# Gated FFN on one core: x loaded in halves of the model dimension, first weights in small pieces in order of use

## The chip, the cores and the metric

The kernel runs on one core of a Trainium2 chip. A core has a matrix engine (TensorE, PE in the profile), a vector engine (VectorE, DVE), a scalar engine (ScalarE, ACT), GpSimd (POOL) and a sync engine (SP). Each runs its own program in order, and they wait for each other on semaphores. Transfers between HBM and the on-chip memory (SBUF) are issued by SP, ACT or POOL, and are carried out by 16 DMA engines. Matrix products go into PSUM, eight banks of 512 fp32 columns on 128 partitions.

The metric is the device time of one execution in microseconds (us). Before the change it is 301.58 us, the median of three runs (301.4 to 301.84).

## The reference

A gated feed-forward layer in bf16: 1024 tokens (B x S = 32 x 32), model dimension D = 1024, hidden dimension F = 3584.

```python
def reference(x, w_gate, w_up, w_down):
    return (_gelu(x @ w_gate) * (x @ w_up)) @ w_down
```

`_gelu` is the tanh approximation. x is 2 MB; the three weights are 7.3 MB each.

## The kernel before

**Layout.** D is cut into 8 pieces of 128 (`dk`), F into 28 chunks of 128 (`m`). PE needs the contraction on the partitions, so x has to be transposed (`xT`); weights are used as they lie. The rows of D are dealt to partitions as d = 8p + k: partition p of piece k holds row 8p + k of the weights, and x is transposed to match.

**x.** x arrives in three pieces by tokens, A (0 to 256), B (256 to 512) and C (512 to 1024). `load_x` (L263) loads a piece in four DMAs, one for each quarter of D on its own 32 partitions, in rows of 256 elements (512 bytes). Two quarters go by SP's queue and two by ACT's. The staging area `xs` lies in the part of `hT` that is written last. DVE then makes each `dk` piece of `xT` with one 32x32-block transpose (L402), which reads every eighth element. It can't begin before both queues have delivered the piece.

**First weights.** Chunks 0 to 7 of both weights (`wgbig`, `wubig`) come row by row (L269): k = 0 and 1 as 128 x 512 pieces, shared between the queues, k = 2 to 7 as 128 x 1024, gate on SP and up on ACT. `early_loads` writes the order: A, weights k = 0 to 7, B, C; 16 DMAs on each queue. On ACT these issues stand ahead of every GELU in the program; only the load of the function's table and one small activation are ahead of them.

**Later weights.** `load_w` (L257) loads groups of four chunks, 1 MB each, gate by SP and up by POOL. `gate_w` holds each until its buffer is free; the first group waits for the whole of x. `issue_wd` (L251) loads `w_down` in the same two programs.

**Order on PE.** Nine dummy matmuls on constants (L324) run first. Then PE goes through *parts* (L345): a part is one chunk m with one stretch of tokens, and needs 8 gate and 8 up matmuls. Parts 0 to 7 are chunks 0 to 7 on tokens A, parts 8 to 15 the same chunks on B, each with 256 columns; gate and up of a part share one PSUM bank (part 8 takes the bank of part 0, and so on). The other 48 have 512 columns. `together` interleaves: for parts 0 to 7 it goes through dk = 0 to 5 for all eight, then finishes them one by one with dk 6 and 7; for parts 8 to 11 it does dk = 0 to 4 for all four, then finishes them; the others go one by one. A matmul waits for its weights, for its transposed x and, where the bank was used, for the product that empties it.

**Order on ACT and DVE.** ACT takes the GELU of the gate half (L383) into one of four buffers. DVE multiplies it with the up half into `hT` (L409); this is called E0, E1 and so on after the part. DVE's order is written out by hand: eight transposes of A, then products and transposes of B and C in the order of `mix`:

`E0 E1 B0 E2 B1 E3 B2 E4 B3 E5 B4 E6 B5 E7 B6 B7 C0 E8 C1 ...`

The second product, hT times `w_down` (L367), follows on PE; ACT and DVE copy its results out in turn (L389, L415) and SP stores them (L313).

Of the kernel before, what the change touches and what calls it, by code (L numbers as in the profile page):

```python
# [5 lines left out]
P = 128  # L6
# [78 lines left out]
def bass_standalone__geglu_ffn__sampling_kernel(  # L85
# [7 lines left out]
    xf = x.flatten_outer_dims()  # L93
# [5 lines left out]
    DK = D // P  # L99
# [21 lines left out]

    XC = N // 32
    XE = D // 4
    XA, XB, XC2 = (0, 256), (256, 512), (512, 1024)
    XPIECES = [XA, XB, XC2]
    W0 = [(0, 0, 512), (0, 512, 1024), (1, 0, 512), (1, 512, 1024)]
    W0 += [(k, 0, 1024) for k in range(2, DK)]

    parts = []
    for t0, t1 in (XA, XB):
# [7 lines left out]
    NPART = len(parts)  # L142
# [10 lines left out]

    steps = []

    def together(ps_, ks):
        for dk in range(ks):
            for key in ("G", "U"):
                for p in ps_:
                    steps.append((p, key, dk))  # L160
        for p in ps_:
            for key in ("G", "U"):
                for dk in range(ks, DK):
                    steps.append((p, key, dk))

    together(range(0, 8), 6)
    together(range(8, 12), 5)
    for p in range(12, NPART):
        together([p], 0)


    dve_order = [("T", dk) + XA for dk in range(DK)]
    mix = "E0 E1 B0 E2 B1 E3 B2 E4 B3 E5 B4 E6 B5 E7 B6 B7 C0 E8 C1 E9 C2 E10 E11 C3 C4 E12 C5 E13 C6 E14 C7 E15"
    for w in mix.split():
        if w[0] == "E":
            dve_order.append(("E", int(w[1:])))
        else:
            dve_order.append(("T", int(w[1:])) + (XB if w[0] == "B" else XC2))
    dve_order += [("E", p) for p in range(NSHORT, NPART)]

    jobs = []
# [14 lines left out]
    wu_r = w_up.rearrange("(p k) f -> p k f", k=DK)  # L196
# [6 lines left out]
    Q_X = {(q, s): _Clock(f"x{i}{s}", 16) for i, q in enumerate(XPIECES) for s in range(2)}  # L203
    Q_W0 = {(w, p): _Clock(f"{w}0k{p[0]}c{p[1]}", 16) for p in W0 for w in ("wg", "wu")}
# [8 lines left out]
    ctx = _Ctx()  # L213

    with ExitStack() as es:
# [38 lines left out]
        def load_w(ew, eng, w, j):  # L254
            c0, gsz, buf = groups[j]
            q = (Q_WG if w == "wg" else Q_WU)[j]
            ctx.set((w, j), ew.do(lambda: eng.dma_start(  # L257
                wbuf(w, buf)[:, :, 0:gsz * P], w_r[w][:, :, c0 * P:(c0 + gsz) * P]), clock=q))

        def load_x(ew, eng, q, side):  # L260
            c0, c1 = q[0] // 32, q[1] // 32
            for a in (2 * side, 2 * side + 1):
                v = ew.do(lambda: eng.dma_start(  # L263
                    xs[32 * a:32 * (a + 1), c0:c1, :], x_r[a, :, c0:c1, :]), clock=Q_X[(q, side)])
            ctx.set(("x", q, side), v)

        def load_w0(ew, eng, w, p):
            k, f0, f1 = p
            ctx.set((w + "0", p), ew.do(lambda: eng.dma_start(  # L269
                big[w][:, k, f0:f1], w_r[w][:, k, f0:f1]), clock=Q_W0[(w, p)]))  # L270

        def early_loads(ew, eng, side):
            load_x(ew, eng, XA, side)
            for k in range(2):
                for w in ("wg", "wu"):
                    load_w0(ew, eng, w, W0[2 * k + side])
            for k in range(2, DK):
                load_w0(ew, eng, ("wg", "wu")[side], W0[2 + k])
            load_x(ew, eng, XB, side)
            load_x(ew, eng, XC2, side)  # L280

        def gate_w(ew, j):
            if war[j] is None:
                for s in range(2):
                    ew.wait(Q_X[(XC2, s)], ctx.get(("x", XC2, s)))
                return -1
            ew.wait(C_PE, ctx.get(("U", last_part[war[j]])))
            return war[j]
# [26 lines left out]
                    osb[:, tc, col0:col0 + ncols]), clock=Q_OUT)  # L315
            sp.wait(Q_OUT, last)

        NDUMMY = 9

        def prog_pe(eng):  # L320
            pe = _Eng(ctx, eng, C_PE)
            v = None
            for i in range(NDUMMY):
                v = pe.do(lambda: eng.matmul(ps[:, 7, :], ones_w, ones_x,  # L324
                                             start=True, stop=True), mark=(i == NDUMMY - 1))
            pe.wait(C_PE, v)
            opened = set()
            for (i, key, dk) in steps:
                m, t0, t1, gs, us = parts[i]
                w, (bank, f0, f1) = ("wg", gs) if key == "G" else ("wu", us)  # L330
                buf, slot, j = slot_of[m]
                if j is None:
                    p = next(p for p in W0 if p[0] == dk and p[1] <= m * P < p[2])
                    pe.wait(Q_W0[(w, p)], ctx.get((w + "0", p)))
# [4 lines left out]
                for q in XPIECES:  # L339
                    if q[0] < t1 and t0 < q[1]:  # L340
                        pe.wait(C_DVE, ctx.get(("T", dk, q)))
# [3 lines left out]
                v = pe.do(lambda: eng.matmul(  # L345
                    ps[:, bank, f0:f1],
                    wbuf(w, buf)[:, dk, slot * P:(slot + 1) * P],
                    xT[:, dk, t0:t1],
                    start=first, stop=last and (key == "U" or gs[0] != us[0]),
                ), mark=last)  # L350
                if last:
                    ctx.set((key, i), v)
            pe.wait(Q_WD_SP, ctx.get("wd_sp_total"))
            pe.wait(Q_WD_POOL, ctx.get("wd_pool_total"))
            bank_last_job = {}
            for ji, (tc, col0, ncols, b) in enumerate(jobs):
                if b in bank_last_job:
                    pj = bank_last_job[b]
                    pe.wait(C_ACT if evac_eng_is_act(pj) else C_DVE, ctx.get(("E", pj)))
                else:  # L360
                    pe.wait(C_DVE, ctx.get(("D", owner[b])))
                bank_last_job[b] = ji
                v = None
                for m in range(FM):
                    pe.wait(C_DVE, ctx.get(("D", last_part[m])))
                    last = (m == FM - 1)
                    v = pe.do(lambda: eng.matmul(  # L367
                        ps[:, b, 0:ncols],
                        hT[:, m, tc * P:(tc + 1) * P],
                        wd[:, m, col0:col0 + ncols],  # L370
                        start=(m == 0), stop=(m == FM - 1),
                    ), mark=last)
                ctx.set(("O", ji), v)
# [18 lines left out]
        def prog_dve(eng):  # L392
            dve = _Eng(ctx, eng, C_DVE)

            for what in dve_order:
                if what[0] == "T":
                    dk, q = what[1], what[2:]
                    for s in range(2):
                        dve.wait(Q_X[(q, s)], ctx.get(("x", q, s)))
                    src = xs[:, q[0] // 32:q[1] // 32, :].rearrange(  # L400
                        "p c (j k) -> p c j k", k=DK)[:, :, :, dk]
                    ctx.set(("T", dk, q), dve.do(lambda: eng.transpose(  # L402
                        xT[:, dk, q[0]:q[1]].rearrange("p (c i) -> p c i", i=32), src)))
                else:
                    i = what[1]
                    m, t0, t1, _gs, (ub, u0, u1) = parts[i]
                    dve.wait(C_ACT, ctx.get(("A", i)))
                    dve.wait(C_PE, ctx.get(("U", i)))
                    ctx.set(("D", i), dve.do(lambda: eng.tensor_tensor(  # L409
                        hT[:, m, t0:t1], t_bufs[i % NTB][:, 0:t1 - t0], ps[:, ub, u0:u1], ALU.mult)))  # L410
# [56 lines left out]
```

## Time and profile before

| What | Value |
|---|---|
| median of three runs | 301.58 us (301.4 to 301.84) |
| the profiled execution | 300.94 us |
| its span, first to last instruction | 299.6 us |
| PE busy | 294.0 us, 98% of the span |
| DVE busy | 60.2 us |
| ACT busy | 41.4 us |
| moved by DMA | 26.43 MB, mean 88 GB/s |
| first 22.5 us: DMA busy tenths of three slices | 8, 9, 9 |
| granted TensorE clock | 1.00 |

In the timeline a row gives the start, the time taken, the engine, the line, the operation with output and input, the count, and in brackets how long the engine was idle before it and what released it. SPq and ACTq rows are the issuing of DMAs, not the transfer. In the table by stretches a row gives the stretch in us, its length, the busy share of PE, PEld, DVE, ACT and POOL with the instructions begun, the TensorE clock, the busy share of the DMA engines (which can pass 1, as transfers on one engine overlap) and their GB/s.

### The profile page before, as it was taken

What the parts mean: (1) busy time and instruction counts of PE and PEld (TensorE: products, weight loads), DVE (VectorE), ACT (ScalarE), POOL (GpSimd) and SP (SyncE); (2) the same over time, 40 slices, a digit from 0 to 9 for tenths busy, and PEclk for the clock granted to TensorE, in tenths of its full rate; (3) what the DMA queues carried; (4) which work ended last, traced back from release to release, by engine and by line L of the source; (5) the groups of instructions that cost most, each with busy time, mean ns of one, the idle gap of its engine ahead of it and who ended that gap; (6) DMA issues with size and microseconds to landing.
All of it is one profiled execution on the core that took longest, in us unless ns stands there. A gap on an engine that the chain in (4) does not pass through costs nothing.

```text
span 299.6 us, 3392 instructions
## 1 busy us (share of the span) xinstructions
PE 294.0 (98%) x1485; PEld 147.6 (49%) x1509; DVE 60.2 (20%) x96; ACT 41.4 (14%) x75; POOL 7.0 (2%) x12
## 2 busy tenths in 40 slices
PE   7999999999999999999999999999999999999997
PEld 3878744444444444444444444444444444444456
DVE  3259811211111211111211112210000000000000
ACT  1042211111211111211111211110000000000000
POOL 0001001020001002000000000000000000000000
DMA  8998002947007400952103000000000100010001
GB/s 239 381 223 270 13 1 81 343 142 278 2 0 251 171 0 7 357 198 63 77 0 142 0 0 2 0 0 18 20 18 18 35 20 18 18 36 19 18 18 37
DMA packets 19118, 26.43 MB, mean 88 GB/s; under 512 B 1056, under 2 KB 13472, under 8 KB 19104
## 3 DMA queue, kind: packets, MB, share of 16 engines
q1 hardware_dynamic: 13344, 14.68, 15.0%
q0 software_dynamic: 2176, 8.39, 7.9%
q10 hardware_dynamic: 3584, 3.15, 3.4%
q8 instruction: 12, 0.20, 0.3%
q14 instruction: 2, 0.02, 0.0%
HBM read 24.12 MB, written 2.10 MB: 87 GB/s over the span
## 4 chain that ended last, share of the span: by engine, by line
PE 97%; DMA 1%; issue 1%; DVE 1%; ACT 0%; DVEq 0%
PE ps L345 64%; PE ps L367 32%; DMA hT<-in_x_dram 1%; DVE xT L402 0%; ACT L377 0%; DVE hT L409 0%; ACT xT L389 0%; DVEq L41 0%
## 5 line engine op out<-in xcount | busy, mean ns | idle before, releaser
L367 PE MATMUL ps<-wd,hT 128*128 128x512 bf16 (+1 forms) x468 | 96.5, 366 | 0.4
L345 PE MATMUL ps<-xT,wgbig 128*128 128x512 bf16 (+1 forms) x378 | 78.6, 343 | 1.8 <-DVE xT L402 0.8
L345 PE MATMUL ps<-xT,wubig 128*128 128x512 bf16 (+1 forms) x379 | 78.8, 343 | 0.3
L367 PEld LDWEIGHTS ps<-wd,hT 128*128 128x128 bf16 x476 | 46.6, 98 | 50.4
L409 DVE TENSOR_TENSOR hT<-tb,ps 128x512 bf16<-128x512 f32 (+1 forms) x64 | 39.1, 613 | 140.8 <-PE ps L345 140.6
L383 ACT ACTIVATE tb<-ps 128x512 f32<-128x512 f32 (+1 forms) x64 | 34.8, 544 | 162.7 <-PE ps L345 161.2
L345 PEld LDWEIGHTS ps<-xT,wgbig 128*128 128x128 bf16 x384 | 37.4, 98 | 34.6 <-PE ps L324 1.7
L345 PEld LDWEIGHTS ps<-xT,wubig 128*128 128x128 bf16 x384 | 37.6, 98 | 31.9 <-DMA wubig<-in_w_up_dram 0.3
L345 PE MATMUL ps<-xT,wgsmall 128*128 128x512 bf16 x126 | 30.1, 379 | 0.1
L345 PE MATMUL ps<-xT,wusmall 128*128 128x512 bf16 x125 | 29.8, 379 | 0.2
L415 DVE CAST xT<-ps 128x512 bf16<-128x512 f32 (+1 forms) x8 | 5.3, 658 | 88.1 <-PE ps L367 88.1
L345 PEld LDWEIGHTS ps<-xT,wusmall 128*128 128x128 bf16 x128 | 12.5, 98 | 15.1
L345 PEld LDWEIGHTS ps<-xT,wgsmall 128*128 128x128 bf16 x128 | 12.5, 98 | 15.1
L402 DVE STREAM_TRANSPOSE xT<-hT 128x256 bf16<-128x256 bf16 (+1 forms) x24 | 17.8, 771 | 5.9 <-DMA hT<-in_x_dram 5.9
L389 ACT ACTIVATE xT<-ps 128x512 bf16<-128x512 f32 (+1 forms) x9 | 5.2, 573 | 93.1 <-PE ps L367 93.1
L324 PE MATMUL ps<-const-bfloat16-1.0 128*128 128x512 bf16 x9 | 4.0, 629 | 0.8 <-PEq L452 0.8
L257 POOL DMA_DIRECT2D wubig<-in_w_up_dram x3 | 2.6, 883 | 64.8 <-PE ps L345 64.8
L257 POOL DMA_DIRECT2D wusmall<-in_w_up_dram x2 | 1.9, 960 | 48.5 <-PE ps L345 26.0
L251 POOL DMA_DIRECT2D wd<-in_w_down_dram x3 | 2.3, 762 | 19.1 <-PE ps L345 19.1
L324 PEld LDWEIGHTS ps<-const-bfloat16-1.0 128*128 128x128 bf16 x9 | 1.2, 141 | 2.7 <-issue 2.7
L377 ACT ACT_TABLE_LOAD x1 | 1.3, 1283 | 0.7 <-PEq L452 0.7
L377 ACT ACTIVATE warm<-const-float32-0.0 128x1 f32<-128x1 f32 x1 | 0.2, 202 | 0.0
(4 smaller groups left out, 0.4 us busy)
## 6 DMA issues: line engine op xcount, KB each, us to landing
wd<-in_w_down_dram SPq DMA_DIRECT2D x4, 1024.0 KB, 10.6
wgbig<-in_w_gate_dram SPq DMA_DIRECT2D x3, 1024.0 KB, 5.6
wubig<-in_w_up_dram POOLq DMA_DIRECT2D x3, 1024.0 KB, 9.5
wd<-in_w_down_dram POOLq DMA_DIRECT2D x3, 1024.0 KB, 10.1
wgsmall<-in_w_gate_dram SPq DMA_DIRECT2D x2, 1024.0 KB, 5.6
wusmall<-in_w_up_dram POOLq DMA_DIRECT2D x2, 1024.0 KB, 8.8
out_dram<-xT SPq DMA_DIRECT2D x15, 128.0 KB, 1.7
wgbig<-in_w_gate_dram SPq DMA_DIRECT2D x6, 256.0 KB, 7.6
```

What stands on the lines that cost most here:

```text
L251: ew.do(lambda: eng.dma_start(wd[:, a:b, :], wd_r[:, a:b, :]), clock=clock)
L257: ctx.set((w, j), ew.do(lambda: eng.dma_start(wbuf(w, buf)[:, :, 0:gsz * P], w_r[w][:, :, c0 * P:(c0 + gsz) * P]), clock=q))
L324: v = pe.do(lambda: eng.matmul(ps[:, 7, :], ones_w, ones_x, start=True, stop=True), mark=(i == NDUMMY - 1))
L345: v = pe.do(lambda: eng.matmul(ps[:, bank, f0:f1], wbuf(w, buf)[:, dk, slot * P:(slot + 1) * P], xT[:, dk, t0:t1], start=first, stop=last ...
L367: v = pe.do(lambda: eng.matmul(ps[:, b, 0:ncols], hT[:, m, tc * P:(tc + 1) * P], wd[:, m, col0:col0 + ncols], start=(m == 0), stop=(m == F ...
L377: act.do(lambda: eng.activation(warm[:, 0:1], const0, ACTF.Gelu_apprx_tanh))
L383: ctx.set(("A", i), act.do(lambda: eng.activation(t_bufs[i % NTB][:, 0:t1 - t0], ps[:, gb, g0:g1], ACTF.Gelu_apprx_tanh)))
L389: ctx.set(("E", ji), act.do(lambda: eng.activation(osb[:, tc, col0:col0 + ncols], ps[:, b, 0:ncols], ACTF.Copy)))
L402: ctx.set(("T", dk, q), dve.do(lambda: eng.transpose(xT[:, dk, q[0]:q[1]].rearrange("p (c i) -> p c i", i=32), src)))
L409: ctx.set(("D", i), dve.do(lambda: eng.tensor_tensor(hT[:, m, t0:t1], t_bufs[i % NTB][:, 0:t1 - t0], ps[:, ub, u0:u1], ALU.mult)))
L415: ctx.set(("E", ji), dve.do(lambda: eng.tensor_copy(osb[:, tc, col0:col0 + ncols], ps[:, b, 0:ncols])))
```

## The change

Five things are changed together.

- Rows of D are dealt in two halves, d = 512 hh + 4p + k: pieces dk = 0 to 3 need only the first half of x's columns, 4 to 7 the second. x comes in six pieces (three stretches of tokens by two halves) in rows of 128 elements, 256 bytes. There are 24 DMAs for x where there were 12.
- The first weights follow a written list, `EARLY`. k = 0 and 1 come in pieces of 512 columns, the first and last of them halved by partitions over both queues; k = 2 to 5 come as whole rows, each halved by partitions (64 x 1024 on each queue); k = 6 and 7 come together in four pieces of 128 x 2 x 512. The second half of A comes between k = 3 and k = 4; B and C come at the end. Each queue issues 27 early DMAs.
- PE's order: for dk 0 and 1, parts 0 to 3 and then 4 to 7; dk 2 to 5 for all eight; then parts 0 to 3 do dk 6 and are finished one by one, and parts 4 to 7 likewise. Parts 8 to 11 do dk 0 to 4 as before.
- DVE's order has four products ahead of the first transpose of B.
- Eight dummy matmuls; `load_w` loads each group in two DMAs.

The core of the diff:

```diff
-    XA, XB, XC2 = (0, 256), (256, 512), (512, 1024)
-    XPIECES = [XA, XB, XC2]
-    W0 = [(0, 0, 512), (0, 512, 1024), (1, 0, 512), (1, 512, 1024)]
-    W0 += [(k, 0, 1024) for k in range(2, DK)]
+    T_A, T_B, T_C = (0, 256), (256, 512), (512, 1024)
+    XPIECES = [t + (hh,) for t in (T_A, T_B, T_C) for hh in range(2)]
+    LO, HI, ALL = (0, 512), (512, 1024), (0, 1024)
+    EARLY = [("x", XPIECES[0]),
+             ("w", "wg", (0, 1), LO, (0, 1)), ("w", "wu", (0, 1), LO, (0,)), ("w", "wg", (0, 1), HI, (1,)),
+             ("w", "wu", (0, 1), HI, (0,)), ("w", "wg", (1, 2), LO, (1,)),
+             ("w", "wu", (1, 2), LO, (0,)), ("w", "wg", (1, 2), HI, (1,)),
+             ("w", "wu", (1, 2), HI, (0, 1))]
+    for k in (2, 3):
+        EARLY += [("w", "wg", (k, k + 1), ALL, (0, 1)), ("w", "wu", (k, k + 1), ALL, (0, 1))]
+    EARLY += [("x", XPIECES[1])]
+    for k in (4, 5):
+        EARLY += [("w", "wg", (k, k + 1), ALL, (0, 1)), ("w", "wu", (k, k + 1), ALL, (0, 1))]
+    EARLY += [("w", "wg", (6, 8), LO, (0,)), ("w", "wu", (6, 8), LO, (1,)),
+              ("w", "wg", (6, 8), HI, (0,)), ("w", "wu", (6, 8), HI, (1,))]
+    EARLY += [("x", q) for q in XPIECES[2:]]
...
-    together(range(0, 8), 6)
-    together(range(8, 12), 5)
-    for p in range(12, NPART):
-        together([p], 0)
-    dve_order = [("T", dk) + XA for dk in range(DK)]
-    mix = "E0 E1 B0 E2 B1 E3 B2 E4 B3 E5 B4 E6 B5 E7 B6 B7 C0 E8 C1 E9 C2 E10 E11 C3 C4 E12 C5 E13 C6 E14 C7 E15"
+    first, second = range(0, 4), range(4, 8)
+    for dk in (0, 1):
+        run(first, [dk])
+        run(second, [dk])
+    run(range(0, 8), range(2, 6))
+    for ps_ in (first, second):
+        run(ps_, [6])
+        for p in ps_:
+            run([p], [7])
+    run(range(8, 12), range(0, 5))
+    for p in range(8, NPART):
+        ks = range(5 if p < 12 else 0, DK)
+        run([p], ks, ("G",))
+        run([p], ks, ("U",))
+    dve_order = []
+    for w in ("A0 A1 A2 A3 A4 A5 A6 A7 E0 E1 E2 E3 B0 B1 E4 B2 E5 B3 E6 E7 B4 B5 B6 B7 "
+              "C0 E8 C1 E9 C2 E10 C3 E11 C4 E12 C5 E13 C6 E14 C7 E15").split():
...
-    x_r = xf.rearrange("(c i) (a e) -> a i c e", i=32, a=4)
-    wg_r = w_gate.rearrange("(p k) f -> p k f", k=DK)
+    x_r = xf.rearrange("(c i) (hh a e) -> hh a i c e", i=32, hh=2, a=4)
+    wg_r = w_gate.rearrange("(hh p k) f -> p hh k f", hh=2, k=KH)
...
         def early_loads(ew, eng, side):
+            for it in EARLY:
+                if it[0] == "x":
+                    t0, t1, hh = q = it[1]
+                    for a in (2 * side, 2 * side + 1):
+                        v = ew.do(lambda: eng.dma_start(
+                            xs[32 * a:32 * (a + 1), t0 // 32:t1 // 32, hh * 128:(hh + 1) * 128],
+                            x_r[hh, a, :, t0 // 32:t1 // 32, :]), clock=Q_X[(q, side)])
+                    ctx.set(("x", q, side), v)
+                elif side in it[4]:
+                    _, w, (k0, k1), (f0, f1), sides = it
+                    p0, p1 = (0, P) if len(sides) == 1 else (64 * side, 64 * side + 64)
+                    ctx.set((it, side), ew.do(lambda: eng.dma_start(
+                        big[w][p0:p1, k0:k1, f0:f1],
+                        w_r[w][p0:p1, k0 // KH, k0 % KH:k0 % KH + k1 - k0, f0:f1]),
+                        clock=Q_W0[(it, side)]))
...
-        NDUMMY = 9
+        NDUMMY = 8
```

`run(ps_, ks, keys)` appends, for each dk in `ks`, the gate matmuls of the parts and then their up matmuls.

More of the change, by code (lines that the diff above doesn't have):

```diff
@@ L120, in bass_standalone__geglu_ffn__sampling_kernel @@
     wd_gate_chunk = [min(FM - 1, 3 + 3 * k) for k in range(len(wd_groups))]
+    KH = DK // 2
     XC = N // 32
     XE = D // 4
-    XA, XB, XC2 = (0, 256), (256, 512), (512, 1024)
-    XPIECES = [XA, XB, XC2]
-    W0 = [(0, 0, 512), (0, 512, 1024), (1, 0, 512), (1, 512, 1024)]
-    W0 += [(k, 0, 1024) for k in range(2, DK)]
+    T_A, T_B, T_C = (0, 256), (256, 512), (512, 1024)
[14 more added lines that the diff above has]
+    EARLY += [("x", q) for q in XPIECES[2:]]
     parts = []
-    for t0, t1 in (XA, XB):
+    for t0, t1 in (T_A, T_B):
         for m in range(NBIG):
@@ L154, in bass_standalone__geglu_ffn__sampling_kernel, with run @@
     steps = []
-    def together(ps_, ks):
-        for dk in range(ks):
-            for key in ("G", "U"):
+    def run(ps_, ks, keys=("G", "U")):
+        for dk in ks:
+            for key in keys:
                 for p in ps_:
                     steps.append((p, key, dk))
-        for p in ps_:
-            for key in ("G", "U"):
-                for dk in range(ks, DK):
-                    steps.append((p, key, dk))
-    together(range(0, 8), 6)
-    together(range(8, 12), 5)
-    for p in range(12, NPART):
-        together([p], 0)
-    dve_order = [("T", dk) + XA for dk in range(DK)]
-    mix = "E0 E1 B0 E2 B1 E3 B2 E4 B3 E5 B4 E6 B5 E7 B6 B7 C0 E8 C1 E9 C2 E10 E11 C3 C4 E12 C5 E13 C6 E14 C7 E15"
-    for w in mix.split():
+    first, second = range(0, 4), range(4, 8)
[5 more added lines that the diff above has]
+        run(ps_, [6])
+        for p in ps_:
+            run([p], [7])
[7 more added lines that the diff above has]
+              "C0 E8 C1 E9 C2 E10 C3 E11 C4 E12 C5 E13 C6 E14 C7 E15").split():
         if w[0] == "E":
@@ L177, in bass_standalone__geglu_ffn__sampling_kernel @@
         else:
-            dve_order.append(("T", int(w[1:])) + (XB if w[0] == "B" else XC2))
+            dve_order.append(("T", int(w[1:])) + {"A": T_A, "B": T_B, "C": T_C}[w[0]])
     dve_order += [("E", p) for p in range(NSHORT, NPART)]
@@ L193, in bass_standalone__geglu_ffn__sampling_kernel @@
     out_r = of.rearrange("(tc p) d -> p tc d", p=P)
-    x_r = xf.rearrange("(c i) (a e) -> a i c e", i=32, a=4)
-    wg_r = w_gate.rearrange("(p k) f -> p k f", k=DK)
-    wu_r = w_up.rearrange("(p k) f -> p k f", k=DK)
+    x_r = xf.rearrange("(c i) (hh a e) -> hh a i c e", i=32, hh=2, a=4)
+    wg_r = w_gate.rearrange("(hh p k) f -> p hh k f", hh=2, k=KH)
+    wu_r = w_up.rearrange("(hh p k) f -> p hh k f", hh=2, k=KH)
     wd_r = w_down.rearrange("(m p) d -> p m d", p=P)
@@ L202, in bass_standalone__geglu_ffn__sampling_kernel @@
     C_POOL = _Clock("pool")
-    Q_X = {(q, s): _Clock(f"x{i}{s}", 16) for i, q in enumerate(XPIECES) for s in range(2)}
-    Q_W0 = {(w, p): _Clock(f"{w}0k{p[0]}c{p[1]}", 16) for p in W0 for w in ("wg", "wu")}
+    Q_X = {(q, e): _Clock(f"x{i}{e}", 16) for i, q in enumerate(XPIECES) for e in range(2)}
+    Q_W0 = {(it, e): _Clock(f"{it[1]}k{it[2][0]}c{it[3][0]}q{e}", 16)
+            for it in EARLY if it[0] == "w" for e in it[4]}
     Q_WG = [_Clock(f"wg{j}", 16) for j in range(NG)]
@@ L256, in load_w @@
             q = (Q_WG if w == "wg" else Q_WU)[j]
[L257 to L270, printed above, removed]
-        def early_loads(ew, eng, side):
[L273 to L280, printed above, removed]
+            for hh in range(2):
+                v = ew.do(lambda: eng.dma_start(
+                    wbuf(w, buf)[:, hh * KH:(hh + 1) * KH, 0:gsz * P],
+                    w_r[w][:, hh, :, c0 * P:(c0 + gsz) * P]), clock=q)
@@ new lines, in load_w @@
+            ctx.set((w, j), v)
+        def early_loads(ew, eng, side):
+            for it in EARLY:
[13 more added lines that the diff above has]
+                        clock=Q_W0[(it, side)]))
@@ L282, in gate_w @@
         def gate_w(ew, j):
             if war[j] is None:
-                for s in range(2):
-                    ew.wait(Q_X[(XC2, s)], ctx.get(("x", XC2, s)))
+                for e in range(2):
+                    ew.wait(Q_X[(XPIECES[-1], e)], ctx.get(("x", XPIECES[-1], e)))
                 return -1
@@ L332, in prog_pe @@
                 if j is None:
-                    p = next(p for p in W0 if p[0] == dk and p[1] <= m * P < p[2])
-                    pe.wait(Q_W0[(w, p)], ctx.get((w + "0", p)))
+                    it = next(it for it in EARLY if it[0] == "w" and it[1] == w
+                              and it[2][0] <= dk < it[2][1] and it[3][0] <= m * P < it[3][1])
+                    for e in it[4]:
+                        pe.wait(Q_W0[(it, e)], ctx.get((it, e)))
                 else:
@@ L338, in prog_pe @@
                     pe.wait(C_DVE, ctx.get(("D", bank_before[i][bank])))
-                for q in XPIECES:
-                    if q[0] < t1 and t0 < q[1]:
-                        pe.wait(C_DVE, ctx.get(("T", dk, q)))
+                for t in (T_A, T_B, T_C):
+                    if t[0] < t1 and t0 < t[1]:
+                        pe.wait(C_DVE, ctx.get(("T", dk, t)))
                 first = (i, bank) not in opened
@@ L396, in prog_dve @@
                 if what[0] == "T":
[L397 to L403, printed above, removed]
+                    dk, (t0, t1) = what[1], what[2:]
+                    q = (t0, t1, dk // KH)
+                    for e in range(2):
+                        dve.wait(Q_X[(q, e)], ctx.get(("x", q, e)))
+                    o = (dk // KH) * 128
+                    src = xs[:, t0 // 32:t1 // 32, o:o + 128].rearrange(
+                        "p c (j k) -> p c j k", k=KH)[:, :, :, dk % KH]
+                    ctx.set(("T", dk, (t0, t1)), dve.do(lambda: eng.transpose(
+                        xT[:, dk, t0:t1].rearrange("p (c i) -> p c i", i=32), src)))
                 else:
```

## The prediction

> **What bounds the kernel now.** I read the page's busy times and slices first, then the chain of waits, then the first 26 us of the timeline, then the DMA issues of x by their line, and last the DMA rate microsecond by microsecond.
>
> ```profile
> span 299.6 us, 3392 instructions
> PE 294.0 (98%) x1485; PEld 147.6 (49%) x1509; DVE 60.2 (20%) x96; ACT 41.4 (14%) x75; POOL 7.0 (2%) x12
> PE   7999999999999999999999999999999999999997
> DMA  8998002947007400952103000000000100010001
> PE ps L345 64%; PE ps L367 32%; DMA hT<-in_x_dram 1%; DVE xT L402 0%; ACT L377 0%; DVE hT L409 0%; ACT xT L389 0%; DVEq L41 0%
> ```
>
> PE sets the time. The chain is matmuls for 96%, and whatever this change does must show where PE is not yet running or stops. The DMA engines are nearly full in the first three slices (22 us): that is where the edits lie.
>
> ```profile
> 0.78 4.00 PE L324 MATMUL ps<-const-bfloat16-1.0 128*128 128x512 bf16 x9 [0.78 <-PEq L452]
> 4.83 4.27 DVE L402 STREAM_TRANSPOSE xT<-hT 128x256 bf16<-128x256 bf16 x8 [4.83 <-DMA hT<-in_x_dram]
> 5.60 1.03 PE L345 MATMUL ps<-xT,wgbig 128*128 128x256 bf16 x8 [0.82 <-DVE xT L402]
> 6.46 5.52 SPq L263 DMA_DIRECT2D hT<-in_x_dram  x4
> 6.61 5.89 ACTq L263 DMA_DIRECT2D hT<-in_x_dram  x4
> 16.86 2.57 ACT L383 ACTIVATE tb<-ps 128x256 f32<-128x256 f32 x6 [14.63 <-PE ps L345]
> 17.28 0.86 DVE L409 TENSOR_TENSOR hT<-tb,ps 128x256 bf16<-128x256 f32 x2 [8.19 <-PE ps L345]
> 19.19 0.64 DVE L402 STREAM_TRANSPOSE xT<-hT 128x256 bf16<-128x256 bf16 x1 [1.06 <-DMA hT<-in_x_dram]
> 19.98 0.50 PE L345 MATMUL ps<-xT,wgbig 128*128 128x256 bf16 x3
> 25.63 0.49 PE L345 MATMUL ps<-xT,wubig 128*128 128x256 bf16 x3
> ```
>
> The real work starts at 5.60, after the first transpose. Groups of eight 256-column matmuls follow 0.87 us apart, 109 ns a matmul. The second quarter of x (B) is transposed from 19.19, PE stops for it in pieces, and the last three matmuls of part 8 start at 25.63; the next part follows at 25.95. From there PE has no gap to the end, so **the end of part 8 is the mark**: what moves it moves the whole span. From 5.60 to 25.95 PE starts 174 such matmuls (128 of parts 0 to 7, 5 x 8 of parts 8 to 11, 6 more of part 8), 19.0 us; 1.4 us are stalls. With the 5.60 that is all there is to win.
>
> ```profile
> L263 SPq DMA_DIRECT2D hT<-in_x_dram x6: 383/442/4060, 0.7 to 7.9; - x6
> L263 ACTq DMA_DIRECT2D hT<-in_x_dram x6: 390/475/4405, 0.8 to 8.1; - x6
> ```
>
> The durations (min, median, max in ns) of the x issues: most take 0.44 to 0.48 us, the last one on each queue over 4. The issuing engine is held by it. In before this hurts nobody: ACT is free at 12.5 and first needed at 16.86.
>
> ```profile
> 5.00:6.00 1.00, 0.40 (x4) 0.40 (x5) 1.00 (x3) 0.00 (x0) 0.00 (x0) 1.00 1.08 351
> 8.00:9.00 1.00, 1.00 (x12) 0.90 (x10) 1.00 (x3) 0.00 (x0) 0.00 (x0) 1.00 1.06 385
> ...
> 17.00:18.00 1.00, 1.00 (x12) 0.90 (x10) 0.70 (x2) 0.89 (x3) 0.00 (x0) 1.00 1.14 289
> ```
>
> The last number is GB/s, for rows of 1 KB, 2 KB and 512 bytes. Over 16 engines that is 47, 85 and 28 ns a row.
>
> **The change, part by part.** *Shorter x rows.* No row of 256 bytes is in the trace. If only bytes cost, one takes 14 ns; if only the count costs, 28. From 1 KB to 512 bytes 19 ns are saved, so another 256 off saves about 9: I take 19 ns, and keep 14 and 28. The Trainium skill (DMA: Bandwidth & Descriptors, Specifications) says that line rate needs 512 bytes and that below it the engine does read-modify-write; by that 28 would be the floor of the price, and the time the upper end below. No run here shows it yet.
>
> *The start.* The first piece is 1024 rows of 256 bytes instead of 512: 1024 x 9 / 16 = 0.6 us less, so the first transpose starts at 4.25 and PE at 5.0. Eight dummies instead of nine end 0.44 earlier (4.00 / 9), at 4.3, and do not hold it. The first weights are issued third on both queues and follow the rows; they land sooner than before too. Gain 0.6 us at the start, if it reaches the mark.
>
> *Weights in between.* With part order and pieces changed, PE asks for k0 at 5.0, k1 at 6.7, k2 at 8.5, k3 at 10.2, k4 at 12.0, k6 at 15.5. Bytes up to the second half of A are 2.62 MB, which before had moved by 9.7 us (adding the rates up); the shorter rows make it 10.3, DVE has them 1.1 later (A before: moved by 3.75, first transpose 4.83) and needs 0.64, so PE gets k4 at about 12.2: a stall of 0.2. PE finishes parts 0 to 7 at 5.0 + 128 x 0.109 + 0.2 = 19.2. k6 and k7 now come in 1 KB rows: 1024 x 47 - 512 x 85 ns, over 16, is +0.27 us of DMA time.
>
> *More issues.* Each queue issues 27 early DMAs for 16. At 0.48 us a piece that alone would free ACT at 0.8 + 13.0 = 13.8, before it is needed. But the two long issues must be explained. Rows on one queue before: 512 (A) + 512 (k0, k1) + 768 (k2 to k7) + 512 (B) + 1024 (C) = 3328. The rates add up to 1.98 MB moved by 8.0 and 3.45 MB by 12.0, half on each queue. So about 1690 rows were still open when the last-but-one issue had gone through unhindered, 2200 with the last one, and that one was let go at some 1820 (12.0 and 12.5). Bytes can't be the limit (1.87 MB open passed freely, 1.4 MB held), nor the count of DMAs (9 open passed, 7 held). I read it as a limit of about **1820 open rows a queue**. After the change a queue has 512 + 512 + 256 + 512 + 256 + 512 + 512 + 512 + 1024 + 1024 = 5632 rows, x counting twice. The last issue goes when 5632 - 1820 = 3812 are moved: all up to B (3584), and 228 of the first 1024 of C.
>
> *When is that?* Before, the same bytes up to B (5.24 MB) had moved by 17.0. Added: x rows 4096 x 19 - 2048 x 28 ns, over 16, +1.28; 1 KB rows +0.27; 228 of 1024 rows of a half of C (2048 x 19 / 16 = 2.43), +0.54. That is 19.1. Before, B's rows had moved by 17.0 but its last completion came at 19.10 while all others were in by 18.3; one engine was 0.8 late, just after a 16 KB fetch of instructions began at 16.7. PE comes to the same instructions at about the same time, so I take the 0.8 in: **ACT is free at 19.9** (17.7 with 14 ns and no lag, 22.4 with 28 and the lag).
>
> *Who waits for it.* The sixteen GELUs stand behind the issues in ACT's program. The first could run at 17.1 (part 0 is done 11.6 + 0.2 us after PE's start, 0.3 more to ACT) and runs at 19.95. The first product follows 0.42 later (16.86 to 17.28). DVE's new order has four products ahead of the first B transpose, 0.33 each when they queue: B starts at 19.95 + 0.42 + 1.32 = 21.7 instead of 19.19, though it landed long before. From there to B7: 7 transposes at 0.56 and 4 products at 0.29 (pitches of before) to its start, 0.64 its run, 0.13 to PE, 4 matmuls at 0.109: 6.3 us (6.8 before; two products fewer lie between). Part 8 ends at 28.0 for 25.95.
>
> The sum: +2.0 us. The gain of 0.6 at the start is inside it, spent in waiting. Bounds: 17.7 gives 19.5 + 6.3 = 25.8, -0.2; 22.4 gives 30.5, +4.6. *Nothing for the rest:* part 16 wants the last transpose of C at some 38.5, and C is through DVE about 1 us before; the later loads wait for the last of x, 25 instead of 22.5 us, for use from 62 on; splitting them adds five issues each on SP and POOL, which idle for tens of us. The profiled run had 300.94 us about a span of 299.6; the median is 0.6 above it. I add the 2.0 to the median: **303.6 us**.
>
> **Rivals.** *The issues are not held by rows* (a limit that shorter rows do not fill). ACT is free at 13.8, products start at 17.5, B's first half can start between 18.85 (after four products) and 19.4 (with the lag), part 8 ends at 25.1 to 25.7: 0.8 to 0.2 less, say **301.0**, not slower. The two identical holds speak against it; it decides if ACT is free before 17.
>
> *Held, but short rows are cheap* (14 ns, no lag): **301.4**, the same within what can be told. The small step from 1 KB to 512 bytes speaks against 14 ns.
>
> *The clock falls.* PE would stand from 19.2 to 22.5. Its longest idle stretch before, 0.82 us, cost no clock; the nine dummies at the start ran at 0.44 us for the 0.216 of 512 columns later, for 4.0 us. If the stop brings that state back, 4 us at half rate lose 2.0, less 0.25 of slack against DVE: **305.3**. The Trainium skill (TensorE: Matmul & The Clock Gate, Part 1) puts the drop at an idle window of about 3.4 us; by that a stop of 3.3 us would just escape and the time be the forecast's.
>
> **How the numbers follow.** Chances: the forecast 0.62, cold clock 0.12, cheap rows 0.11, no hold 0.15. 0.2% (0.6 us) is about what a measurement here tells from no change. Of the no-hold case, 0.12 is faster and 0.03 the same: faster 0.12, same 0.14, slower 0.74. The range goes from 300.8, inside the no-hold case, to 305.6, which takes in the cold clock and leaves out the dearest rows with the lag.
>
> **What would show it.** In the profile after: the last x issue on ACT lasting to nearly 20 us, the first GELU right after it with ACT's idle time not put down to PE, B's transposes after four products at about 21.7, PE stopped for some 3 us before part 8; a DMA rate near 16 x 256 / 19 = 215 GB/s in the x stretches. Wrong if ACT is done issuing before 17 us, or if that rate is far from 215.

## The result and the profile after

The changed kernel takes **304.07 us** (median of four runs, 303.45 to 304.88) against 301.49 us (301.36 to 301.84) for the kernel before on the same chip: a ratio of 1.0085, 95% interval 1.0058 to 1.0113. It is slower, by 2.6 us. In a later comparison the same program had 1.0055 (1.0041 to 1.0069), 1.7 us. The profiled execution took 304.88 us, the slowest of the four, about a span of 303.6 us, so its gaps are larger than the median's. One range below reaches up to 305.71 us: that execution was in a slower state, and the ratios leave it out.

The page after: span, busy time by engine, the slices of PE and DMA, and the chain by line.

```profile
span 303.6 us, 3454 instructions
PE 295.9 (97%) x1508; PEld 146.7 (48%) x1508; DVE 54.4 (18%) x96; ACT 40.7 (13%) x75; POOL 10.1 (3%) x17
PE   7897999999999999999999999999999999999997
DMA  7997700839103800780303000000000000010001
PE ps L368 60%; PE ps L390 32%; DMA wgbig<-in_w_gate_dram 3%; SPq L298 3%; SPq L291 1%; DVE hT L434 0%; DVE xT L427 0%; ACT xT L412 0%; DVEq L41 0%
```

From slice 5 on PE is as full as before. The loss is all in the first 30 us, and the full stretch of DMA, which ended near 21 us before, now ends near 27. First weights and their issues stand in the chain, where before there was next to nothing but matmuls.

The first 30 us of the timeline after (columns as before: start, time, engine, line, operation, count, idle time and releaser):

```profile
0.78 3.57 PE L345 MATMUL ps<-const-bfloat16-1.0 128*128 128x512 bf16 x8 [0.78 <-PEq L477]
5.17 0.60 PE L368 MATMUL ps<-xT,wgbig 128*128 128x256 bf16 x4 [0.83 <-DVE xT L427]
11.96 10.53 ACTq L291 DMA_DIRECT2D hT<-in_x_dram  x8
14.23 1.42 DVE L427 STREAM_TRANSPOSE xT<-hT 128x256 bf16<-128x256 bf16 x4 [9.12 <-DMA hT<-in_x_dram]
14.82 1.03 PE L368 MATMUL ps<-xT,wgbig 128*128 128x256 bf16 x8 [0.90 <-DMA wgbig<-in_w_gate_dram]
22.54 2.32 ACT L406 ACTIVATE tb<-ps 128x256 f32<-128x256 f32 x8 [20.31 <-issue]
22.95 1.42 DVE L434 TENSOR_TENSOR hT<-tb,ps 128x256 bf16<-128x256 f32 x4 [7.30 <-ACT tb L406]
24.29 0.76 DVE L427 STREAM_TRANSPOSE xT<-hT 128x256 bf16<-128x256 bf16 x2
24.87 0.60 PE L368 MATMUL ps<-xT,wgbig 128*128 128x256 bf16 x4 [1.54 <-DVE xT L427]
29.89 0.49 PE L368 MATMUL ps<-xT,wgbig 128*128 128x256 bf16 x3
```

Read it against the rows of before. PE starts 0.43 us earlier. ACT's x issues end at 22.49, and the first GELU starts 0.05 later; its idle time is put down to issuing, not to PE. Part 0 had issued its last matmul at 20.24. Four products follow, then B's transposes, then PE goes on with parts 8 to 11. B's first half had landed at 22.97 by its semaphores in the trace, so B's transposes started 1.3 us later than its data allowed. Part 9's last stretch, which follows the end of part 8, starts at 29.89; before it was 25.95. That is 3.94 of the 4.0 us between the two spans.

The x issues by line (min, median, max in ns; first and last start):

```profile
L291 SPq DMA_DIRECT2D hT<-in_x_dram x12: 387/526/3243, 0.7 to 21.3; - x12
L291 ACTq DMA_DIRECT2D hT<-in_x_dram x12: 400/544/3042, 0.8 to 21.4; - x12
```

The last issue starts at 21.4, for 8.1 before. No single one lasts as long as the 4.4 us of before: the hold is spread over the issues of B and C, which are let go one after the other. Three stretches of the table by microseconds (last column GB/s):

```profile
8.00:9.00 1.00, 1.00 (x10) 0.76 (x9) 0.00 (x0) 0.00 (x0) 0.00 (x0) 1.00 1.05 260
12.00:13.00 1.00, 0.93 (x10) 0.62 (x8) 0.00 (x0) 0.00 (x0) 0.00 (x0) 1.00 1.14 261
21.00:22.00 1.00, 0.76 (x8) 0.54 (x7) 0.00 (x0) 0.00 (x0) 0.00 (x0) 1.00 1.35 215
```

At 21 to 22 us only 256-byte rows move: 215 GB/s is 19 ns a row. At 8 to 9 us it is weights in 2 KB rows. Before, such rows moved at 385 GB/s; here it is 260, though the engines are as busy (1.05). That was not in the prediction.

### The profile page after: what moved, and what is told of

It is laid out like the page before. It is cut to its first block, busy times and chain, and to the rows that moved or that the text cites. A ratio compares the mean times of both kernels' runs of the same rounds, so it can differ in the third digit from the quotient of the medians.

```text
span 303.6 us, 3454 instructions
## 1 busy us (share of the span) xinstructions
PE 295.9 (97%) x1508; PEld 146.7 (48%) x1508; DVE 54.4 (18%) x96; ACT 40.7 (13%) x75; POOL 10.1 (3%) x17
## 4 chain that ended last, share of the span: by engine, by line
PE 92%; DMA 3%; SPq 3%; issue 0%; DVE 0%; ACT 0%; DVEq 0%
PE ps L368 60%; PE ps L390 32%; DMA wgbig<-in_w_gate_dram 3%; SPq L298 3%; SPq L291 1%; DVE hT L434 0%; DVE xT L427 0%; ACT xT L412 0%; DVEq L41 0%
## 5 line engine op out<-in xcount | busy, mean ns | idle before, releaser
L406 ACT ACTIVATE tb<-ps 128x512 f32<-128x512 f32 (+1 forms) x64 | 34.0, 546 | 167.4 <-PE ps L368 147.1
L368 PEld LDWEIGHTS ps<-xT,wusmall 128*128 128x128 bf16 x128 | 12.5, 98 | 15.1
L368 PEld LDWEIGHTS ps<-xT,wgsmall 128*128 128x128 bf16 x128 | 12.5, 98 | 15.1
L427 DVE STREAM_TRANSPOSE xT<-hT 128x256 bf16<-128x256 bf16 (+1 forms) x24 | 11.4, 509 | 12.8 <-DMA hT<-in_x_dram 12.8
L281 POOL DMA_DIRECT2D wubig<-in_w_up_dram x6 | 4.5, 748 | 61.3 <-PE ps L368 61.3
L281 POOL DMA_DIRECT2D wusmall<-in_w_up_dram x4 | 3.1, 784 | 53.6 <-DMA hT<-in_x_dram 28.2
```

Of the source, the lines that this page charges most:

```text
L281: v = ew.do(lambda: eng.dma_start(wbuf(w, buf)[:, hh * KH:(hh + 1) * KH, 0:gsz * P], w_r[w][:, hh, :, c0 * P:(c0 + gsz) * P]), clock=q)
L368: v = pe.do(lambda: eng.matmul(ps[:, bank, f0:f1], wbuf(w, buf)[:, dk, slot * P:(slot + 1) * P], xT[:, dk, t0:t1], start=first, stop=last ...
L406: ctx.set(("A", i), act.do(lambda: eng.activation(t_bufs[i % NTB][:, 0:t1 - t0], ps[:, gb, g0:g1], ACTF.Gelu_apprx_tanh)))
L427: ctx.set(("T", dk, (t0, t1)), dve.do(lambda: eng.transpose(xT[:, dk, t0:t1].rearrange("p (c i) -> p c i", i=32), src)))
```

## The experiments

Three suspects: the hold of ACT by its own issues, the weights halved by partitions, and the short rows of x. Each ratio is to the kernel before, run beside it.

### Weights whole again in the changed kernel

The line stands twice, for k = 2, 3 and for k = 4, 5:

```diff
-        EARLY += [("w", "wg", (k, k + 1), ALL, (0, 1)), ("w", "wu", (k, k + 1), ALL, (0, 1))]
+        EARLY += [("w", "wg", (k, k + 1), ALL, (0,)), ("w", "wu", (k, k + 1), ALL, (1,))]
```

> The changed kernel, with the weights of k = 2 to 5 no longer halved by partitions: gate whole (128 x 1024) on SP, up whole on ACT. Theory (halving makes a 2 KB row dear: 265 GB/s from 8 to 16 us is 124 ns a row, for 85 before): 1024 rows at 39 ns less over 16 engines, so the stretch is 2.5 us shorter and runs at about 385 GB/s, ACT is let go at 20.0 instead of 22.5, part 8 ends near 27.4 instead of 29.9: about 301.6 to 302. Rival (the slow stretch comes from the 256-byte rows around it, or from the order of the pieces): the rate stays near 265 and the time near 304.

304.16 us (303.52 to 305.27), ratio 1.0086 (1.0055 to 1.0118). The theory's rate came in part (2 KB rows took 95 ns on average, for 125 in the first profile), its time did not. Two stretches of weights:

```profile
8.00:9.00 1.00, 1.00 (x7) 0.74 (x5) 0.00 (x0) 0.00 (x0) 0.00 (x0) 1.00 1.01 363
13.00:14.00 1.00, 1.00 (x12) 0.83 (x9) 0.00 (x0) 0.00 (x0) 0.00 (x0) 1.00 1.06 376
```

From 10 to 12 us it was 261 and 291 GB/s, with the short rows of A's second half among the weights. The bytes up to B had moved by 19.5, but ACT was let go only at 21.04, with 1567 rows of its queue open. One of the 16 shares of each load came 1 to 2 us after the others from 11 us on (weights up, k = 2: fifteen by 9.3, the last at 11.3). A hold that waits for the slowest DMA engine would eat what the faster weights gained; that is argued from the landings, and why one engine was late is open. So this run does not show what the halves cost in the changed kernel.

### ACT's part of C issued by SP

```diff
-                    for a in (2 * side, 2 * side + 1):
+                    whose = (side,) if t0 < 512 else ((0, 1) if side == 0 else ())
+                    for s in whose:
+                        for a in (2 * s, 2 * s + 1):
...
```

> The changed kernel, with ACT's half of x's last piece C (4 DMAs, 2048 rows) issued by SP behind its own, so that ACT's queue is left 3584 rows and its last issue goes once 1764 are moved, at about 13.5 us. Theory (the hold of ACT is on the path): the first GELU follows part 0's last matmul, at about 20.6 instead of 22.54, B's transposes start when B has landed, at about 23.0 instead of 24.29, part 8 ends some 1.2 us earlier: about 302.8. Rival (the slow transfers alone set the end and the hold is beside them): first GELU earlier but the same 304.

302.30 us (301.09 to 303.3), ratio 1.0020 (1.0001 to 1.0039). Most of the loss is gone.

```profile
11.96 2.11 ACTq L293 DMA_DIRECT2D hT<-in_x_dram  x4
19.89 1.21 ACT L408 ACTIVATE tb<-ps 128x256 f32<-128x256 f32 x4 [17.66 <-PE ps L370]
22.18 0.77 DVE L429 STREAM_TRANSPOSE xT<-hT 128x256 bf16<-128x256 bf16 x2 [0.46 <-DMA hT<-in_x_dram]
```

ACT is through at 14.1, its first GELU waits for PE again, and B's transposes wait for B, no longer for products. The weights are still halved here: the hold was the part that cost most. (In this profile the halved rows took 106 ns on average.)

### Both edits

> Both of the last two edits. Theory (halving and the hold are the whole loss; the short rows cost 1.5 us of transfer that is mostly paid by the earlier start and by the faster transposes seen in the changed kernel, 0.36 us apart instead of 0.53): PE starts at 5.1, ends parts 0 to 7 near 19.3, the first half of B is there at 18.5 to 19.5, part 8 ends at 24.5 to 25.3 for 25.95 before: 300.1 to 300.9, faster than before. Rival (the short rows themselves make it slow): above 302.

302.44 us (301.86 to 303.11), ratio 1.0023 (1.0008 to 1.0038): not faster than before, and no better than moving C alone. In the profile PE started at 5.92 with matmuls 213 ns apart, and the first half of B on its second queue was complete at 21.67, fifteen of its engines at 19.9. Two candidates for the rest, then: cold matmuls, or B.

### The same with eleven dummy matmuls

> The changed kernel with whole weights for k = 2 to 5, C's ACT half on SP, and eleven dummy matmuls for eight. In the profile of the same kernel with eight, the first twelve matmuls started 213 ns apart, for 109 later, and one DMA engine delivered B 1.8 us after the others. Theory (cold matmuls cost it 1.3 us, and the late engine belonged to that execution): no 213 ns starts, B's first half at about 20, part 8 ends at 25 to 25.5: 300.8 to 301.5. Rival (it is bound by B, which comes later because of the short rows, and a warm PE only waits longer): still 302 to 302.7.

302.81 us (301.42 to 303.91), ratio 1.0032 (1.0017 to 1.0047). PE was warm after three matmuls, and the time is the same. The rival holds as far as this form waits for B, whose transposes began at 22.1; that the short rows make B late is not shown. Fifteen of the sixteen engines had brought B's first half by 20.3, the last at 22.04, as far as the landings tell. In all three profiles of the changed kernel with whole weights one engine brought B 1.6 to 1.8 us after the others, so the late engine did not belong to one execution. Why it was late is open.

### Short rows alone, in the kernel before

```diff
-                v = ew.do(lambda: eng.dma_start(
-                    xs[32 * a:32 * (a + 1), c0:c1, :], x_r[a, :, c0:c1, :]), clock=Q_X[(q, side)])
+                for e0, e1 in ([(0, XE)] if q == XA else [(0, XE // 2), (XE // 2, XE)]):
+                    v = ew.do(lambda: eng.dma_start(
+                        xs[32 * a:32 * (a + 1), c0:c1, e0:e1], x_r[a, :, c0:c1, e0:e1]), clock=Q_X[(q, side)])
```

> The kernel before, with only the rows of B and C cut to 256 bytes (each of these DMAs split in two by columns, same layout, same order). Theory (a queue takes no more than about 1820 open rows): a queue has 4864 rows, the last issue on ACT goes after 3044 are moved: 15.0 + 2.4 for B + 0.5 of C = 18.0, up to 18.8 with one engine late, instead of 12.5; the first GELU moves from 16.86 to then, part 8 ends 0 to 0.8 later: 301.5 to 302.3. Rival (the hold goes by bytes or by the count of DMAs): by bytes ACT is free at 12.5 as before; the first GELU stays at 16.9 and only B's later landing can be seen.

302.19 us (301.15 to 305.71), ratio 1.0020 (1.0001 to 1.0039).

```profile
7.18 11.43 ACTq L264 DMA_DIRECT2D hT<-in_x_dram  x8
18.65 1.98 ACT L384 ACTIVATE tb<-ps 128x256 f32<-128x256 f32 x6 [16.42 <-PE ps L346]
```

No byte more is loaded, only more rows, and ACT is let go at 18.60 instead of 12.5. The limit by rows had said 18.0 to 18.8; limits by bytes or by the count of DMAs are out: 1946 rows were open, in some four DMAs and 0.50 MB, where before some 1820 were, in seven DMAs and 1.4 MB. (The profile names PE as the releaser of the GELU; the issue ended at 18.60, 0.05 before it.)

### Short rows without the hold

As the last one, with ACT's part of C issued by SP.

> The kernel before with the rows of B and C cut to 256 bytes, and ACT's half of C issued by SP, so that ACT is not held. With short rows and the hold the ratio was 1.0020 and the first GELU at 18.65. Theory (in that kernel the later landing of B was the cost, not the hold): the first GELU at 16.9 again, and the time the same, ratio 1.000 to 1.003. Rival (the hold was the cost): ratio 1.000 or below.

302.33 us (301.69 to 305.07), ratio 1.0031 (1.0011 to 1.0050). ACT was free at 11.0, and the time is no better: in this kernel the rows cost some 0.2 to 0.3% and the hold nothing that can be told from it. The first GELU came at 19.45, not 16.9, since PE began at 6.67 in that execution and ran cold to about 9.8.

### Weights halved by partitions, alone, in the kernel before

```diff
-                load_w0(ew, eng, ("wg", "wu")[side], W0[2 + k])
+                for w in ("wg", "wu"):
+                    load_w0(ew, eng, w, W0[2 + k], side, 64 * side, 64 * side + 64)
...
```

> The kernel before, with only the weights of k = 2 to 7 halved by partitions: each queue issues 64 x 1024 of gate and of up, 12 issues for 6 on each queue. Theory (halving makes a 2 KB row dear, 124 ns for 85, as in the profile of the changed kernel): 1536 rows x 39 / 16 = 3.7 us more before B, transposes of B start near 23 and part 8 ends some 3 us later: about 305. Rival (making the same weights whole did not lower the median of the changed kernel, 304.16 for 304.07, so halving as such costs little and the slow rate belonged to that execution): 301.6 to 302.4, with 2 KB rows at 85 to 100 ns.

302.92 us (302.82 to 303.47), ratio 1.0036 (1.0023 to 1.0048). Rows of 2 KB took 121 ns on average (89 before), and from 8 to 14 us the rate was 248 to 258 GB/s in every stretch:

```profile
10.00:11.00 1.00, 1.00 (x12) 0.88 (x11) 0.00 (x0) 0.00 (x0) 0.00 (x0) 1.00 1.08 248
11.00:12.00 1.00, 1.00 (x12) 0.90 (x10) 0.00 (x0) 0.00 (x0) 0.00 (x0) 1.00 1.06 248
```

So halving is slow by itself, in a second kernel. But the rate isn't fixed: from 14 to 18 us, once both queues had issued everything (14.2 and 14.6), the same rows moved at 320 to 326 GB/s. What changed there was not tested. B's transposes began at 21.09 for 19.19: 1.9 us, not 3.7. Here B's engines all ended within 0.1 us, with no late one; the fetch of instructions that in before began at 16.7, just ahead of the late engine, came at 23.7. That the fetch makes an engine late is not shown: in the changed kernel with whole weights one was late from 11 us on, with no fetch near.

### Halved by columns instead

Against the kernel halved by partitions (the comment is added here):

```diff
-                    load_w0(ew, eng, w, W0[2 + k], side, 64 * side, 64 * side + 64)
+                    load_w0(ew, eng, w, W0[2 + k], side)   # columns 512 * side to 512 * side + 512
...
```

> The kernel before with the weights of k = 2 to 7 halved by columns instead of by partitions: each queue issues 128 x 512 of gate and of up, the same count of DMAs and bytes as in the kernel halved by partitions (ratio 1.0036, 121 ns a row). Theory (it is the 64 partitions that are slow): 1 KB rows at about 47 ns, 3072 x 47 - 1536 x 85 over 16 = 0.9 us later for B, ratio 1.000 to 1.003, transfers of 8 to 14 us near 350 GB/s. Rival (twice as many DMAs on two queues is what is slow): near 260 GB/s and 1.0036 or more.

301.65 us (301.23 to 302.82), ratio 1.0003 (0.9989 to 1.0017).

```profile
10.00:11.00 1.00, 1.00 (x12) 0.90 (x10) 0.00 (x0) 0.00 (x0) 0.00 (x0) 1.00 1.10 344
11.00:12.00 1.00, 1.00 (x12) 0.90 (x10) 0.00 (x0) 0.00 (x0) 0.00 (x0) 1.00 1.10 348
```

The same count of DMAs, the same bytes, shorter rows, and no loss: it is the 64 partitions that are slow, not the doubled count. (A DMA of 64 partitions also has only 64 rows here; no run tells the two apart.)

### The same half on both queues

Gate on SP and up on ACT, each as partitions 0 to 63 and then 64 to 127.

> As the last one, but both queues carry the same half of the partitions at the same time: SP loads gate, first partitions 0 to 63 and then 64 to 127, ACT up in the same way. If halved transfers are slow because rows meet in too few partitions, this is the worst case and slower than the kernel with one half on each queue: above 305. If 64-partition DMAs are merely small (fewer rows each, more issues), the two kernels are alike. If halving costs little in both, 301.6 to 302.4.

306.39 us (305.02 to 307.29), ratio 1.0142 (1.0117 to 1.0167), worse than one half on each queue. But a row took 129 ns on average, hardly more than 121, and the rate from 9 to 13 us was 252 to 256 GB/s, so this run does not say that rows meeting in few partitions are the cause. Four times the loss for 8 ns a row comes from the order too: PE stopped at 10.8 and 13.0, and for 1.6 us at 19.3, each time for weights by their landings, and began part 9 some 2 us later than with one half on each queue. What makes a 64-partition DMA slow stays open.

### The order of products and transposes in the kernel before

```diff
-    mix = "E0 E1 B0 E2 B1 E3 B2 E4 B3 E5 B4 E6 B5 E7 B6 B7 C0 E8 ...
+    mix = "E0 E1 E2 E3 B0 B1 B2 B3 B4 B5 B6 B7 E4 E5 E6 E7 C0 E8 ...
```

> The kernel before with DVE's order alone changed: products E0 to E3 ahead of B's first transpose, all eight of B, then E4 to E7. In the profile of before E2 stood behind B's wait, and PE lost 1.4 us in four stalls, three of them from 19.6 on, as products stood between B's transposes (0.86 us a pair, PE uses 0.87 for a dk). Theory: B's transposes start at 19.2 as before and follow 0.56 apart, PE goes on at 19.98 without a stall, part 8 ends at about 25.0 for 25.95: 0.9 us faster, 300.6 to 301.0. Rival (B landing ends the wait, and E0 to E3 finish after it, so that B starts later): no gain.

301.22 us (300.75 to 301.95), ratio 0.9982 (0.9969 to 0.9994): faster, by less than hoped. B landed at 19.77 in that execution, 0.7 us later than in the profile of before.

### That order, and eleven dummies

> The kernel before with the order of products and B transposes that gained 0.18%, and eleven dummies for nine. Theory (some executions start cold, as in two of the profiles of kernels with nine dummies; the eleven end at 5.0, before the first real matmul at 5.6): 0 to 0.5 us less than with the order alone, ratio 0.9965 to 0.9982. Rival (cold starts are rare or hidden by the wait for B): ratio 0.998 again.

**300.62 us** (300.21 to 302.23), ratio 0.9969 (0.9953 to 0.9985): the fastest of all, though its interval overlaps that of the order alone, so what the dummies add is not shown.

```profile
17.82 1.73 DVE L409 TENSOR_TENSOR hT<-tb,ps 128x256 bf16<-128x256 f32 x4 [8.80 <-PE ps L345]
19.47 4.29 DVE L402 STREAM_TRANSPOSE xT<-hT 128x256 bf16<-128x256 bf16 x8
23.68 1.38 DVE L409 TENSOR_TENSOR hT<-tb,ps 128x256 bf16<-128x256 f32 x4
```

Products, then all of B in one go, then products. PE has no stop of over 0.35 us in it; the GELU of part 8 starts at 25.49, for 26.15 before.

### The changed kernel again

> The changed kernel once more, beside the others of this call. If its transfers of 8 to 16 us again run near 265 GB/s, the halved weights are slow in every execution; if they come near 330 or more, the first profile was an unlucky one. ACT is let go when 3812 rows of its queue are moved in either case, at 20.5 to 22.5, and the time is 303.5 to 304.5.

303.65 us (302.94 to 304.08), ratio 1.0055 (1.0041 to 1.0069).

```profile
11.00:12.00 1.00, 1.00 (x11) 0.90 (x10) 0.00 (x0) 0.00 (x0) 0.00 (x0) 1.00 1.25 244
11.96 9.20 ACTq L291 DMA_DIRECT2D hT<-in_x_dram  x8
13.76 1.43 DVE L427 STREAM_TRANSPOSE xT<-hT 128x256 bf16<-128x256 bf16 x4 [8.17 <-DMA hT<-in_x_dram]
21.21 2.32 ACT L406 ACTIVATE tb<-ps 128x256 f32<-128x256 f32 x8 [18.98 <-PE ps L368]
22.95 0.76 DVE L427 STREAM_TRANSPOSE xT<-hT 128x256 bf16<-128x256 bf16 x2
28.76 0.38 ACT L406 ACTIVATE tb<-ps 128x256 f32<-128x256 f32 x1 [5.23 <-PE ps L368]
```

(The first line is of the table by stretches, the others of the timeline.) The last is the GELU of part 8, which in the timeline of before is this row:

```profile
26.15 0.38 ACT L383 ACTIVATE tb<-ps 128x256 f32<-128x256 f32 x1 [4.70 <-PE ps L345]
```

The slow weights are there again, 120 ns a row, and so is the hold, to 21.16. Part 0 had issued its last matmul at 19.20, and B's first half had landed at 21.28, so B's transposes at 22.95 started 1.7 us later than its data allowed. The span is 302.2, 2.6 above that of the profile of before. That profile was a fast one of its kernel (300.94, 0.6 below the median), and beside the runs of its own comparison this kernel lost 1.7 us at the median. The steps below go by this execution.

## Why the prediction was right, and where its terms were off

The forecast was 303.6 us; 304.07 was measured, +2.6 us for the forecast +2.0, and +1.7 in the second comparison. The mechanism is the one forecast, and shown: ACT's GELUs stood behind its own issues, the issues were let go by rows moved, B's transposes stood behind four products, and PE stopped for them. Taking the hold away by itself brought the ratio from 1.0085 (1.0055 in the second comparison) down to 1.0020. That the order of DVE takes part is read from the timeline; no run put B's transposes ahead of the products in the changed kernel.

Point by point:

- *Short rows at 19 ns:* 205 to 230 GB/s in the x stretches, 18 to 20 ns. Right. The Trainium skill's rule (DMA: Bandwidth & Descriptors, Specifications) of read-modify-write below 512 bytes would have made 28 the floor; for these loads into SBUF no such price shows.
- *The limit of 1820 open rows:* 1855 rows of ACT's queue were open when it was let go in the first profile, 1946 with short rows alone; but 2096 in the second profile of the changed kernel and 1567 where one engine was late. Where the last DMA on ACT has 256 rows and not 512, it was 1514 to 1654. Right as a rule by rows, rough as a number.
- *ACT free at 19.9:* it was 21.2 (22.5 in the first profile). **This term was mis-sized.** It priced the weights of k = 2 to 5 at 85 ns a row, as if a DMA of 64 partitions moved like one of 128. They took 120 (125 in the first profile): 1024 rows x 35 ns / 16 = 2.2 us of transfer. So the second half of A was transposed from 13.8 (14.2 in the first profile, where PE stood 1.2 us, by the profile for the gate weights of k = 4), not from 11.4. That the halves alone moved the release is not shown: with whole weights, and one engine late, it came at 21.04. The Trainium skill has a rule on halves (DMA: Bandwidth & Descriptors, Rules for kernel authors): two transfers to disjoint partition halves are not worth it, as both use all the engines. The runs in the kernel before agree and go further: 1.0036 by partitions, 1.0003 by columns.
- *B there long before, and PE through with parts 0 to 7 at 19.2:* PE was through at 21.7 in the second profile and 23.2 in the first, since it waited for weights (and in the second started at half rate, below). B's first half landed at 21.28 and 22.97, 1.3 to 1.7 us ahead of its first transpose, not long before. So PE stood 1.8 to 1.9 us (start to start), where some 3 were forecast.
- *6.3 us from B's first transpose to the end of part 8:* 5.6. **This term was too long.** Transposes of 256 columns followed 0.33 to 0.37 us apart when queued (1.42 for four, with the run of the last; 4.27 for eight before, 0.53 apart), so that PE was not held between them. The price was taken from before, where they read every eighth element and not every fourth.
- *The sum:* 21.2 + 1.8 + 5.6 = 28.6, and the GELU of part 8 started at 28.76 for 26.15: +2.6. The forecast had 19.9 + 1.8 + 6.3. Two errors, of +1.3 and -0.7, in part cancel: that its +2.0 came close is partly luck.
- *The start:* 0.43 us earlier (0.66 in the second profile) for 0.6, and all of it lost in the waits, as forecast.

Of the rivals, *no hold* is out. *Cheap rows* is out at 19 ns. *The clock falls* was not put to the test: the stop lasted 1.8 to 1.9 us, not 3.3, and PE went on at 109 ns a matmul.

How the loss divides among hold, halves and short rows is only partly settled. Alone in the kernel before, halves cost 0.36% and short rows 0.20 to 0.31%. In the changed kernel whole weights gave nothing, neither with the hold (1.0086) nor without it (1.0023 for 1.0020), though with them fifteen of the sixteen engines had brought B's first half by 19.7 to 20.3, for 21.3 to 22.3 with halves. The one late engine took that back, so what the halves cost there stays open. With hold and halves gone, 0.2 to 0.3% is left, about the price of short rows alone. What remains after that of the earlier start and the faster transposes could not be told apart.

## What to carry to other kernels

An issue of a DMA is an instruction of the engine that issues it, and blocks what stands behind it when its queue is full. Count the rows that a queue has open, not the bytes: when ACT's last issue was let go, 1514 to 2096 rows were open in these profiles, but anything from 0.4 to 1.4 MB. Keep the last, big, unhurried loads off the queue of an engine that has work to do.
Split a load by columns, or by whole pieces, rather than by partitions (1.0003 for 1.0036 here).
Where one engine serves two streams, put the part whose data is there ahead of the part that still has to land, and the stream that the critical engine waits for in one go: that order alone made the kernel before faster (0.9982). It helps only if nothing holds the first part up, as the hold did with the products of the changed kernel.

## What the runs showed that was not expected

- A load of 64 partitions x 2 KB moved at about 250 GB/s on two queues while these were still issuing (320 to 326 later), one of 128 partitions x 1 KB at 344 to 365, in the same place of the same kernel.
- A transpose on DVE that reads every fourth bf16 element takes 0.33 to 0.37 us for 256 columns, start to start, one that reads every eighth 0.53. That the step is the cause is not shown, as the layout changed with it.
- PE's first real matmuls ran at half rate, 213 ns apart, in six of the twelve profiles with eight or nine dummies, for 12 to 18 matmuls (up to 1.9 us). They did so with eight and with nine, and the same program did it in one profile and not in the other. The clock column showed 0.50 in one of the six and 1.00 in the other five. The second profile of the changed kernel shows it by the time of its first matmuls, four in 1.01 us, where the first profile had 0.60:

```profile
4.93 1.01 PE L368 MATMUL ps<-xT,wgbig 128*128 128x256 bf16 x4 [0.59 <-DVE xT L427]
5.95 1.04 PE L368 MATMUL ps<-xT,wubig 128*128 128x256 bf16 x4
```

In the changed kernel the hold covered this loss: in the second profile part 0 was done near 19.3 even so, and ACT was let go at 21.16. In the form without the hold, warming PE brought nothing, as B was what it waited for.
